# Seven output tiles on all 128 rows of the array, and batch 1's first transposes behind batch 0's last copies, in a fused attention and GeGLU kernel on one core

## Chip, cores, metric

One core of a Trainium2 chip. The metric is the device time of one execution in microseconds; less is better. In the profile's lines PE stands for TensorE's matmuls, PEld for its weight loads, DVE for VectorE and ACT for ScalarE; the span is the time from the first to the last instruction of the profiled execution, and a bank is the piece of accumulation memory that a group of matmuls fills before an engine copies it out.

## The reference, cut to what matters

```python
# q, k, v: (8, 12, 448, 64); w_gate, w_val: (768, 1536); w_out: (1536, 768)
scores = matmul(q, k.T) / sqrt(64)
x = matmul(maximum(scores, 0) ** 2 / 448, v)   # then (8 * 448, 768)
out = (gelu(x @ w_gate) * (x @ w_val)) @ w_out # (3584, 768), float32
```

## The kernel before: the parts that matter

The kernel lays out all work beforehand. Each piece is an `Op` with an engine, a planned cost and what it waits for; `run_plan` then issues the pieces in the order that the plan gives. TensorE has two queues in the plan: `PE0`, the lower 64 rows of the array, and `PE1`, the upper 64. On the chip they are one stream of instructions.

```python
def mm(o, lhsT, rhs, row, col, start, stop):           # a 64*64 tile of the array
    return nc.tensor.matmul(o, lhsT, rhs, start=start, stop=stop,
                            tile_position=(P * row, P * col))     # P = 64

def both(at, ops, step=0.0):         # lower and upper at the same time
    for i, (lo, hi) in enumerate(ops):
        lower.append((at + i * step, lo)); pairs.append(("with", lo, hi))

def then(at, step, los, his, done):  # the upper half of a bank after its lower half
    for i, lo in enumerate(los):
        lower.append((at + i * step, lo))
    pairs.append(("then", los[-1], his))
    bank_of[los[-1]] = done
```

The gate, value and output matmuls contract over 128 rows, but do it in two halves: the lower 64 rows accumulate into a bank, and when they are through, the upper 64 add theirs to the same bank, while the lower rows go on with the next bank. So at any time four 64*64 tiles can be at work on two banks. The upper rows lag by a bank or so. An output tile (128 of the 3584 rows, `FC` = 12 contraction steps, two column groups of 384):

```python
def emit(r, fc):
    if not box:
        box[0] = new_bank(cp)
    i, o = divmod(fc, WOG)
    if r == 1 and fc == 0:
        wait_lower(box)
    for j, (b, c) in enumerate(chunks):
        ins = mm(box[0][HALF[j], 0:N], uT[b][HALF[r], fc, c * P:(c + 1) * P],
                 wo[i][HALF[r], o, cols], r, j, r == 0 and fc == 0, r == 1 and fc == FC - 1)
    box[1] = ins
# ... [cut: the copy to osb on ACT, the stores]
ops = [[Op(f"PE{r}", step, lambda r=r, fc=fc: emit(r, fc), ...) for fc in range(FC)] for r in range(2)]
then(at, step, *ops, cp)
```

And where the upper halves go in the order:

```python
for kind, lo, hi in pairs:
    if kind == "with":
        upper.append((tau[place[lo]], hi))
    else:
        behind = place[lo] + 1
        # ... [cut: at least 0.3 us of lower work in between]
        hi[0].after = PE0[behind]
        t = tau[behind + 1]
        for i, op in enumerate(hi):
            if i:
                op.after = hi[i - 1]
            upper.append((t, op))
            t += op.cost
upper.sort(key=lambda w: w[0])
```

Attention is spread over this as scores (`sp`, 64*64 tiles), relu on ACT, square on VectorE, and products with v. For batches 0 and 1 q and k are transposed on TensorE by 128*64 tiles (line 334), and copied to `qkT` by VectorE. In the first batch, short of work, TensorE runs fillers of 128*128 (line 296).

## Time and profile before

| | before |
|---|---|
| median time | 430.91 us (430.79 to 432.42, 3 runs) |
| span of the profiled run | 428.7 us |
| TensorE busy | 419.9 us, 98% |
| from the span's start to batch 0's first gate matmul | 27.6 us |
| from there to batch 7's first gate matmul | 346.9 us |
| from there to the end ("the tail") | 54.2 us |

The last three rows cut the span at two instructions: the first gate matmul of batch 0 and that of batch 7. They are stages: start, middle, tail.

### The profile page before, as it was taken

Reading aid. Unit: us, or ns where it says so; the run is one execution under the profiler, and the core shown is the slowest. Engines: PE = TensorE matmul, PEld = TensorE weight load, DVE = VectorE, ACT = ScalarE, POOL = GpSimd, SP = SyncE. Lnnn points to the kernel's source line nnn. Section 1 sums busy time; section 2 is a strip of 40 time slices with the busy share of each in tenths; the row PEclk is TensorE's granted clock in tenths of the full one; section 3 lists DMA queues with packets and bytes.
Section 4 is the critical chain, followed back from the end, with each engine's and each line's share of the span. In section 5 each row is a group of like instructions: output and inputs, shape, how many; then the busy total and the mean of one; then the engine's idle time right before and its main releaser. Section 6 shows DMA issues by size and latency. Waiting matters only on the chain.

```text
span 428.7 us, 19594 instructions
## 1 busy us (share of the span) xinstructions
PE 419.9 (98%) x9091; PEld 359.7 (84%) x9094; DVE 211.1 (49%) x343; ACT 224.5 (52%) x323; POOL 71.6 (17%) x117
## 2 busy tenths in 40 slices
PE   8999999899999999999999999999999999999995
PEld 3559778678898888989999988979999978977895
DVE  3966666167544674347633675346633555212200
ACT  5937563366655555556455565565555565222221
POOL 8655420123001130023100230012200000000000
PEclk9999999999999999999999999999999999999999
DMA  8999999999434796379923699358932100220034
GB/s 109 196 199 198 202 208 185 185 134 140 73 84 90 93 151 75 75 109 140 127 58 95 89 133 118 76 85 109 151 71 77 38 4 3 53 63 3 2 78 112
DMA packets 75377, 44.91 MB, mean 105 GB/s; under 512 B 36128, under 2 KB 71840, under 8 KB 75296
## 3 DMA queue, kind: packets, MB, share of 16 engines
q0 software_dynamic: 37088, 24.39, 43.2%
q1 hardware_dynamic: 37968, 19.08, 26.2%
q8 instruction: 71, 1.16, 1.1%
q10 hardware_dynamic: 240, 0.20, 0.2%
q14 instruction: 10, 0.08, 0.1%
HBM read 48.76 MB, written 11.01 MB: 139 GB/s over the span
## 4 chain that ended last, share of the span: by engine, by line
PE 94%; DVE 2%; ACT 1%; issue 1%; DMA 1%; ACTq 0%; POOL 0%; POOLq 0%
PE ff L159 85%; PE sp L159 7%; ACT rl L381 1%; PE ff L296 1%; PE sp L334 1%; DMA qk<-in_k_dram 1%; DVE attnT L387 1%; DVE xT L437 1%; PE ff L334 0%; DVE qkT L338 0%; ACT osb L532 0%; ACTq L537 0%; POOL qk L211 0%; POOL table L148 0%; ACTq L381 0%
## 5 line engine op out<-in xcount | busy, mean ns | idle before, releaser
L159 PE MATMUL ff<-xT,wg 64*64 64x448 bf16 x2304 | 218.8, 349 | 0.2 <-DVE xT L437 0.2
L159 PE MATMUL ff<-xT,wv 64*64 64x448 bf16 x2304 | 217.6, 349 | 1.4 <-issue 1.4
L381 ACT ACTIVATE rl<-sp 128x896 bf16<-128x896 f32 x168 | 152.3, 918 | 98.2 <-PE sp L159 80.9
L159 PE MATMUL ff<-wo,uT 64*64 64x384 bf16 (+1 forms) x2736 | 150.6, 320 | 0.0
L159 PEld LDWEIGHTS <-wv 64*64 64x64 bf16 x2304 | 126.5, 107 | 18.4 <-issue 3.9
L387 DVE TENSOR_TENSOR attnT<-rl 128x896 bf16<-128x896 bf16 x168 | 104.0, 623 | 74.3 <-ACT rl L381 72.8
L159 PEld LDWEIGHTS <-wg 64*64 64x64 bf16 x2304 | 126.4, 107 | 16.3 <-issue 1.2
L159 PEld LDWEIGHTS <-uT 64*64 64x64 bf16 x2736 | 124.7, 107 | 5.3 <-issue 0.2
L159 PE MATMUL sp<-qkT 64*64 64x448 bf16 (+1 forms) x768 | 107.9, 328 | 0.6 <-ACT rl L381 0.4
L481 DVE TENSOR_TENSOR uT<-gel,ff 128x448 bf16<-128x448 bf16 x96 | 59.5, 620 | 77.0 <-PE ff L159 66.4
L159 PE MATMUL ff<-attnT,v 64*64 64x448 bf16 (+1 forms) x768 | 85.8, 327 | 0.1
L476 ACT ACTIVATE gel<-ff 128x448 bf16<-128x448 f32 x96 | 52.1, 543 | 51.2 <-PE ff L159 50.2
L532 ACT COPY osb<-ff 128x384 f32<-128x384 f32 (+1 forms) x57 | 26.8, 471 | 50.8 <-PE ff L159 47.6
L159 PEld LDWEIGHTS <-qkT 64*64 64x64 bf16 x768 | 43.1, 106 | 10.0 <-issue 3.8
L159 PEld LDWEIGHTS <-v 64*64 64x64 bf16 x768 | 44.6, 107 | 5.5 <-issue 1.2
L437 DVE TENSOR_SCALAR xT<-ff 128x448 bf16<-128x448 f32 x48 | 29.9, 623 | 32.0 <-PE ff L159 31.8
L211 POOL DMA_DIRECT2D qk<-in_q_dram x25 | 15.6, 622 | 152.5 <-DVE uT L481 146.0
L224 POOL DMA_DIRECT2D v<-in_v_dram x44 | 27.3, 628 | 32.7 <-DVE uT L481 24.0
L211 POOL DMA_DIRECT2D qk<-in_k_dram x25 | 15.4, 615 | 41.4 <-DVE uT L481 29.7
L258 DVE COPY qkr<-qk 128x1792 bf16<-128x1792 bf16 x18 | 19.3, 1078 | 0.0
L334 PEld LDWEIGHTS <-qk 128*64 128x64 bf16 x168 | 5.0, 109 | 3.0 <-issue 2.7
L338 DVE COPY qkT<-ff 128x896 bf16<-128x896 bf16 x6 | 3.7, 621 | 6.1 <-PE ff L334 6.1
(22 smaller groups left out, 39.5 us busy)
## 6 DMA issues: line engine op xcount, KB each, us to landing
out_dram<-osb SPq DMA_DIRECT2D x54, 192.0 KB, 2.7
v<-in_v_dram POOLq DMA_DIRECT2D x42, 128.0 KB, 6.2
qk<-in_q_dram POOLq DMA_DIRECT2D x23, 224.0 KB, 4.7
qk<-in_k_dram POOLq DMA_DIRECT2D x23, 224.0 KB, 5.0
wg<-in_moe_w_gate_dram POOLq DMA_DIRECT2D x6, 384.0 KB, 10.4
wv<-in_moe_w_val_dram POOLq DMA_DIRECT2D x6, 384.0 KB, 11.6
wo<-in_moe_w_out_dram POOLq DMA_DIRECT2D x4, 576.0 KB, 14.9
v<-in_v_dram POOLq DMA_DIRECT2D x2, 384.0 KB, 10.7
```

The lines of the kernel that those rows point to most:

```text
L159: return nc.tensor.matmul(o, lhsT, rhs, start=start, stop=stop, tile_position=(P * row, P * col))
L211: op = load(4 * (h1 - h0) * S * D, lambda: nc.gpsimd.dma_start(tile_of().rearrange("p (h x) -> p h x", h=H)[:, h0:h1, :], src[b, h0:h1].re ...
L224: return nc.gpsimd.dma_start(v16[b][HALF[i], h0:h1, :, :], v[b, h0:h1].rearrange("h (p c) d -> p h c d", c=SC)[:, :, c0:c0 + VC, :])
L258: nc.vector.tensor_copy(qkr[b][:, m], qk16[b].rearrange("p (h c d) -> p c h d", c=SC, d=D)[:, :, 4 * m:4 * m + 4])
L296: nc.tensor.matmul(t[:, :], warm[:, 0:128], warm[:, :], start=True, stop=True)
L334: nc.tensor.transpose(t[HALF[j], c, :], src[:, 2 * (2 * m + r) + j, c, :], ident[:, :], tile_position=(0, P * j))
L381: nc.scalar.activation(rl[:, :, :], box[0][:, :, 0:S], AF.Relu)
L387: nc.vector.tensor_tensor(a[:, :, :], box[1][:, :, :], box[1][:, :, :], op=ALU.mult)
L437: nc.vector.tensor_scalar_mul(xT[b][:, pr, :], box[0][:, 0:S], scalar1=out_scale)
L476: nc.scalar.activation(gel[b, fc][:, :], box[0][:, 0:S], AF.Gelu)
L481: u_op[b, fc].ins = nc.vector.tensor_tensor(uT[b][:, fc, :], gel.pop((b, fc))[:, :], box[0][:, 0:S], op=ALU.mult).ins
L532: nc.scalar.copy(ob[:, cols], box[0][:, 0:N])
```

## The change

Its intent: where no attention work stands beside the output tiles, an output matmul can use all 128 rows at once. This halves its instructions, needs no lag between halves, and lets a bank be finished and copied at once. And batch 1's first transposes, whose copies VectorE made between batch 0's last copies, come 3 us later, while batch 0's own transposes come a little earlier.

```diff
+        def emit_full(fc):
+            if not box:
+                box[0] = new_bank(cp)
+            i, o = divmod(fc, WOG)
+            for j, (b, c) in enumerate(chunks):
+                nc.tensor.matmul(box[0][HALF[j], 0:N], uT[b][:, fc, c * P:(c + 1) * P],
+                                 wo[i][:, o, cols], start=fc == 0, stop=fc == FC - 1,
+                                 tile_position=(0, P * j))
+        full = 0 < t < SC // 2 or 2 * t + 2 > SC * (B - 1) - 2      # tiles 1, 2 and 23 to 27
+        if full:
+            ops = [[Op("PE0", step, lambda fc=fc: emit_full(fc), ...) for fc in range(FC)],
+                   [Op("PE1", step, lambda: None) for _ in range(FC)]]
+            for lo, hi in zip(*ops):
+                hi.after = lo
 ... [cut: else as before]
-        then(at, step, *ops, cp)
+        if full:
+            both(at, zip(*ops), step)
+        else:
+            then(at, step, *ops, cp)
-    LO1 = 2.0
+    LO1 = 5.0
-                    x = (1.5 * step if rs == (1,) else -3.0) if b == 0 else -5.0 if m else -2.0
+                    x = ((0.5 if m else 1.5) * step if rs == (1,) else -4.6) if b == 0 else -5.0 if m else -2.0
```

More of the change, by code (lines that the diff above doesn't have):

```diff
@@ L537, in emit_store @@
             engine.dma_start(rows[c, :, cols], osb[t][HALF[j], cols])
-        ops = [[Op(f"PE{r}", step, lambda r=r, fc=fc: emit(r, fc),
+        def emit_full(fc):
[8 more added lines that the diff above has]
+        if full:
+            ops = [[Op("PE0", step, lambda fc=fc: emit_full(fc),
+                       [wo_op[fc // WOG], *(u_op[b, fc] for b, _ in chunks),
+                        *(ring_dep() if fc == 0 else ())], lag=0.24)
+                    for fc in range(FC)],
+                   [Op("PE1", step, lambda: None) for _ in range(FC)]]
+            for lo, hi in zip(*ops):
+                hi.after = lo
+        else:
+            ops = [[Op(f"PE{r}", step, lambda r=r, fc=fc: emit(r, fc),
                    [wo_op[fc // WOG], *(u_op[b, fc] for b, _ in chunks),
@@ L542, in add_out @@
                 for fc in range(FC)] for r in range(2)]
-        cp = Op("ACT", 0.48, emit_copy, [ops[1][-1]], prio=1)
+        cp = Op("ACT", 0.48, emit_copy, [ops[0 if full else 1][-1]], prio=1)
         ring.append(cp)
@@ L551, in add_out @@
                       for j in range(2))
-        then(at, step, *ops, cp)
+        if full:
+            both(at, zip(*ops), step)
+        else:
+            then(at, step, *ops, cp)
     for h0, h1 in ((0, 2), (2, 4), (4, 8), (8, 12)):
```

## The prediction

> **What bounds the kernel now.** I read the page first: its span, busy shares and chain of waits say which engine sets the time.
>
> ```profile
> span 428.7 us, 19594 instructions
> PE 419.9 (98%) x9091; PEld 359.7 (84%) x9094; DVE 211.1 (49%) x343; ACT 224.5 (52%) x323; POOL 71.6 (17%) x117
> ...
> PE ff L159 85%; PE sp L159 7%; ACT rl L381 1%; PE ff L296 1%; PE sp L334 1%; DMA qk<-in_k_dram 1%; DVE attnT L387 1%; DVE xT L437 1%; PE ff L334 0%; DVE qkT L338 0%; ACT osb L532 0%; ACTq L537 0%; POOL qk L211 0%; POOL table L148 0%; ACTq L381 0%
> ```
>
> TensorE is busy nearly always, and its matmuls are 93% of the chain. So what counts is how the array is packed. Almost every matmul is a 64*64 tile: four fit at once, two on the lower 64 rows and two on the upper. The lower rows run one bank's first half of the contraction while the upper rows run the second half of the bank before. I then asked for groups by shape on TensorE, for what the changed instructions cost today:
>
> ```profile
> L159 PE MATMUL ff<-wo,uT 64*64 64x384 bf16 x2640 | 149.5, 323 | 0.0
> L159 PE MATMUL ff<-wo,uT 64*64 64x192 bf16 x96 | 4.4, 243 | 0.0
> ```
>
> No idle time stands before them. Their cadence shows in the timeline of the tail, where only output tiles run: ACT copies a finished bank every 1.95 us (412.46, 414.41, 416.36), and a bank is 24 lower and 24 upper matmuls side by side. So a step of four matmuls takes 1.95 / 12 = 0.1625 us. The end of that timeline:
>
> ```profile
> 421.76 2.30 PE L159 MATMUL ff<-wo,uT 64*64 64x192 bf16 x45
> 423.23 0.48 ACT L532 COPY osb<-ff 128x384 f32<-128x384 f32 x1 [2.57 <-PE ff L159]
> 423.74 0.56 ACTq L537 DMA_DIRECT2D out_dram<-osb  x1
> 424.34 0.32 ACT L532 COPY osb<-ff 128x192 f32<-128x192 f32 x1 [0.63 <-PE ff L159]
> 424.68 0.50 ACTq L537 DMA_DIRECT2D out_dram<-osb  x1
> 425.22 0.32 ACT L532 COPY osb<-ff 128x192 f32<-128x192 f32 x1 [0.57 <-ACT osb L532]
> ```
>
> The last upper matmuls run alone until 424.06, with half the array empty. The last copy then starts only at 425.22, behind the copy and DMA issue of the piece before it. Last, the few places where the shape of the tile already changes, in the timeline of 25.8 to 28.0 us (start, duration, what):
>
> ```profile
> 25.89 0.48 PE L159 MATMUL ff<-attnT,v 64*64 64x448 bf16 x6
> 26.30 0.58 PE L334 MATMUL sp<-ident,qk 128*64 128x128 bf16 x14
> 26.82 0.38 PE L159 MATMUL ff<-attnT,v 64*64 64x448 bf16 x2
> 27.12 0.58 PE L334 MATMUL sp<-ident,qk 128*64 128x128 bf16 x14
> 27.63 0.38 PE L159 MATMUL ff<-attnT,v 64*64 64x448 bf16 x2
> ```
>
> Here one upper pair of 448 columns stands between two sets of full-row transposes. A pair in a stretch of one shape takes 0.189 us and a transpose pair about 0.055. From the start of the last transpose pair of the first set (26.66 in the records) to the next set is 0.46 us. Of that 0.055 + 0.19 is streaming; the rest, about 0.21, is two changes of shape, and the second pair after a change comes another 0.025 late. I call it 0.12 us per change. The records show 43 such changes, with a median of 0.096 us between the end of one stream and the next start, before the 0.025.
>
> **What the Trainium skill says.** "TensorEngine Tiling (Array Packing)", Key Properties: "Changing tiling mode (not just tile) drains the TensorE". The trace agrees: 0.12 us at each change, between 64*64, 128*64 and 128*128 alike. "TensorE: Matmul & The Clock Gate", the table under "Why this matters for your kernels", says that a matmul of 32 rows takes the time of one of 128. So a full-row pair should take what a half-row pair takes; the trace agrees as far as it can: in the warm-up 128*64 pairs of 512 columns follow each other by 0.216 us, which scaled to 384 is 0.162.
>
> **The change, part by part.** It has three: seven output tiles (1, 2 and 23 to 27) in 128*64; the plan start of batch 1's attention 3 us later, so that its first transposes come after batch 0's last copies; batch 0's transposes a little earlier.
>
> Full rows, streaming: a step of a full tile is two matmuls of 0.1625 us instead of four beside each other in 0.1625 us. The instruction count falls by 360, the streaming time by nothing. So this part can gain only at the edges.
>
> Full rows, changes of shape: this is where I looked hardest. I took both orders of TensorE's instructions and marked each place where the tile's shape changes: 45 before, 121 after. Around tile 1 there are 34 new ones, around tile 2 22, in the tail 22, at the start 2 fewer. The reason is the lag: when a full tile begins, the upper rows still owe a bank, and the planner deals those upper pairs one by one between the full pairs. Tile 23's first steps read: full pair, upper pair of gate, full pair, upper pair of gate, three full pairs, and so on. 76 x 0.12 = +9.1 us, all on the path, since nothing else may run in a change.
>
> Full rows, half-empty array: in such a stretch an upper pair runs alone. Around tile 1 some 15 pairs x 0.1625 = 2.4 us; around tile 2 some 6 x 0.19 = 1.1; in the tail 11 x 0.189 = 2.1, against the final stretch of the kernel before, 22 pairs of 192 columns at some 0.0825 = 1.8, which goes. Together 2.4 + 1.1 + 0.3 = 3.8, of which I take 3.5, as some drains overlap.
>
> The end: with full rows the last three pieces finish one after the other, the last 0.99 us after the one before, so that piece's copy (0.32) and issue (0.50) are done when the last is ready. The 425.22 - 424.06 = 1.16 us from last matmul to last copy shrinks to the 0.28 that a copy takes to see its matmul: -0.9 us.
>
> The start: before, VectorE takes the first two qkT copies of batch 1 (27.75 and 28.82, 0.62 each) between the last xT copies of batch 0 (28.29 and 29.35), and the last gate step waits until 30.02. Between 28.5 and 30.0 each half of the array starts only two pairs. After, these transposes (some 1.1 us with their changes) stand behind, so that step could come some 1.8 us earlier; the 1.1 us is paid later. That nets 0.7 us. The planner puts five fewer fillers of 0.216 in the first batch (17 against 22), so its planned gaps shrink by 1.1 us; I believe most of it, since ACT's relus there show 1.2 us of gaps. Start: -1.5 us.
>
> One more item is luck: at 76.55 us the array stands for 1.15 us for nothing that the profile shows ("issue"). It may go or stay; -0.4 on average.
>
> Sum: 9.1 + 3.5 - 0.9 - 1.5 - 0.4 = +9.8 us. 430.9 + 9.8 = 440.7; I say 440.5, a ratio of 1.022.
>
> **The rivals.** First, the changes of shape are cheaper in this setting: a change may cost only because transposes and fillers wait for other things as well. Then 76 changes at 0.05 are 3.8 us, and the time is about 435. Against it: the 0.092 to 0.119 us gaps are the same for three shapes, for lengths from 128 to 512 columns, and with or without a semaphore. At no cost at all it would be 430.9 + 3.5 - 2.8 = 431.6.
>
> Second, the start gives more than I count, since every microsecond of the attention chain there moves the whole kernel: 3 to 4 us instead of 1.5, thus about 438.5. For it: TensorE is only 93% busy from 20 to 30 us, ACT 51%. Against: TensorE's true idle there is 0.66 us, and the rest must be won from half-empty stretches.
>
> Third, weight loads bind the tail, and half the instructions make it quicker: the load row is 10.00 of 10 us busy from 410 to 420. Against: 0.1625 us per step is what the 128*64 warm-up pairs give per column, with far fewer loads. At best nothing changes.
>
> Fourth, the copies of full banks or the arrival of late uT tiles stall full steps, since they come in tile order without the other half's slack. Tile 24 needs the last uT, whose upper pair stands some 14 full steps earlier (2.3 us, against about 1 us for the product and its wait), so I expect none; if it came, 1 us more.
>
> **Range and chances.** The uncertain terms: 0.12 per change by a fifth, 1.8 us; the half-empty array 1 us; the start 1 us; the stall 0.6. Together some 2.4 us, a little more on the fast side, since the first two rivals both go that way: 436.0 to 443.5. The 2% line is 430.91 x 1.02 = 439.5, under my centre by 1.0: slower by over 2% 0.60, within 2% 0.39. Faster by over 2% would need 8.6 us, and TensorE's idle time in all is 8.8, most of it the launch and the last store: 0.01.
>
> **What would show it.** In the profile after: 128*64 rows for wo,uT with 360 matmuls in place of 720, and around 400 to 415 us alternating single pairs with starts about 0.28 to 0.31 us apart where today they are 0.16; the tail's copies spaced 1.95 us once no gate pair is left; the stretch from batch 1's first gate step to batch 7's last of the same length as before; batch 1's first gate step some 5 us later than today's, batch 2's some 8; the last copy 0.3 us behind the last matmul. Wrong would be: single pairs at 0.16 to 0.19 us between starts, so no cost for a change; or a first gate bank more than 3 us earlier.

## The result, and the profile after

The changed kernel takes 442.0 us (median of 6 runs, 441.15 to 443.22) against 431.5 (6 runs): 1.0244 times, interval 1.0220 to 1.0269, so slower. Ratios here and below are the mean time of one kernel's runs over that of the other's runs of the same rounds, so not quite the ratio of the medians.

The page after: span, busy shares, and the chain of waits by line (other lines left out):

```profile
span 439.6 us, 18865 instructions
PE 431.1 (98%) x8726; PEld 348.9 (79%) x8729; DVE 211.4 (48%) x343; ACT 224.4 (51%) x323; POOL 71.6 (16%) x117
...
PE ff L159 78%; PE sp L159 7%; PE ff L544 7%; DVE attnT L387 2%; DMA qk<-in_k_dram 1%; DVE xT L437 1%; PE sp L334 1%; POOL qk L211 1%; DVE qkT L338 0%; ACT osb L532 0%; PE ff L334 0%; ACTq L537 0%; PE ff L296 0%; ACT rl L381 0%; POOL ident masks.py:199 0%
```

TensorE is "busy" for 98% again, with 365 matmuls fewer and 11 us more. Busy time doesn't show what was lost: a matmul's recorded time (some 323 ns for 384 columns) is about double the 0.1625 us after which the next on the same rows starts, so short gaps between streams vanish in it. The groups by shape show the new instructions, each at nearly the mean duration of the old (332 against 323 ns for 384 columns, 246 against 243 for 192). The old groups are smaller by the 720 that they replace, 624 of 384 columns and all 96 of 192:

```profile
L159 PE MATMUL ff<-wo,uT 64*64 64x384 bf16 x2016 | 121.6, 323 | 0.0
...
L544 PE MATMUL ff<-wo,uT 128*64 128x384 bf16 x312 | 32.8, 332 | 0.0
...
L544 PE MATMUL ff<-wo,uT 128*64 128x192 bf16 x48 | 2.1, 246 | 0.0
```

Where the time is lost shows in the order. The timeline of TensorE after, at the beginning of the tail (start us, duration us, line, what):

```profile
412.05 0.35 PE L544 MATMUL ff<-wo,uT 128*64 128x384 bf16 x2
412.33 0.38 PE L159 MATMUL ff<-xT,wg 64*64 64x448 bf16 x2
412.64 0.35 PE L544 MATMUL ff<-wo,uT 128*64 128x384 bf16 x2
412.92 0.38 PE L159 MATMUL ff<-xT,wg 64*64 64x448 bf16 x2
413.23 0.68 PE L544 MATMUL ff<-wo,uT 128*64 128x384 bf16 x6
413.84 0.38 PE L159 MATMUL ff<-xT,wg 64*64 64x448 bf16 x2
```

A full pair starts 0.28 us before the upper gate pair that follows it, and that one 0.31 us before the next full pair. In a stretch of one shape they would be 0.16 and 0.19 apart, and today's upper gate pair would run beside lower work, not alone. Taken from the records, after 60 us there are 78 changes of shape, with together 8.55 us between the end of one stream and the next start (median 0.116; a stream is taken to last 0.417 ns per column, about the 0.42 at which pairs of one shape follow each other). The kernel before has none there.

The end of the kernel after:

```profile
434.15 0.48 ACT L532 COPY osb<-ff 128x384 f32<-128x384 f32 x1 [1.51 <-PE ff L544]
435.26 0.32 ACT L532 COPY osb<-ff 128x192 f32<-128x192 f32 x1 [0.63 <-PE ff L544]
435.61 0.50 ACTq L537 DMA_DIRECT2D out_dram<-osb  x1
435.98 0.14 PEld L159 LDWEIGHTS <-warm 64*64 64x64 bf16 x4
435.98 0.25 PE L159 MATMUL sp<-warm 64*64 64x64 bf16 x4
436.14 0.32 ACT L532 COPY osb<-ff 128x192 f32<-128x192 f32 x1 [0.57 <-PE ff L544]
```

The last output matmul ends at 436.05 in the records and the last copy starts at 436.14: 0.09 us, where the kernel before had 1.16. Banks finish one after the other, and no copy waits behind another copy's store.

The stages (one profiled execution each; the last column is TensorE's idle after 40 us, in pieces over 0.1 us, that the profile puts down to nothing, "issue"):

| kernel | start | middle | tail | unexplained idle |
|---|---|---|---|---|
| before | 27.6 | 346.9 | 54.16 | 1.4 |
| after | 26.5 | 357.8 | 55.28 | 1.1 |

So the start is 1.1 us shorter, the middle 10.9 us longer and the tail 1.1 us longer. (One execution's start is worth little: the nine traces below and here with the old start have 27.6 to 29.1 us, and the kernel before happens to have the least.)

### The profile page after: what moved, and what is told of

The parts are those of the page before. It is cut to its first block, busy times and chain, and to the rows that moved or that the text cites. A ratio compares the mean times of both kernels' runs of the same rounds, so it can differ in the third digit from the quotient of the medians.

```text
span 439.6 us, 18865 instructions
## 1 busy us (share of the span) xinstructions
PE 431.1 (98%) x8726; PEld 348.9 (79%) x8729; DVE 211.4 (48%) x343; ACT 224.4 (51%) x323; POOL 71.6 (16%) x117
## 4 chain that ended last, share of the span: by engine, by line
PE 93%; DVE 3%; DMA 1%; POOL 1%; issue 1%; ACT 0%; ACTq 0%; POOLq 0%
PE ff L159 78%; PE sp L159 7%; PE ff L544 7%; DVE attnT L387 2%; DMA qk<-in_k_dram 1%; DVE xT L437 1%; PE sp L334 1%; POOL qk L211 1%; DVE qkT L338 0%; ACT osb L532 0%; PE ff L334 0%; ACTq L537 0%; PE ff L296 0%; ACT rl L381 0%; POOL ident masks.py:199 0%
## 5 line engine op out<-in xcount | busy, mean ns | idle before, releaser
L159 PE MATMUL ff<-xT,wg 64*64 64x448 bf16 x2304 | 222.2, 349 | 1.5 <-issue 1.1
L159 PE MATMUL ff<-xT,wv 64*64 64x448 bf16 x2304 | 222.1, 350 | 0.0
L159 PEld LDWEIGHTS <-wv 64*64 64x64 bf16 x2304 | 127.8, 107 | 19.6 <-issue 4.3
L159 PEld LDWEIGHTS <-wg 64*64 64x64 bf16 x2304 | 127.7, 107 | 19.0 <-issue 2.9
L159 PE MATMUL ff<-wo,uT 64*64 64x384 bf16 x2016 | 121.6, 323 | 0.0
L159 PE MATMUL sp<-qkT 64*64 64x448 bf16 (+1 forms) x768 | 106.1, 328 | 0.9 <-ACT rl L381 0.8
L159 PEld LDWEIGHTS <-uT 64*64 64x64 bf16 x2016 | 95.5, 107 | 8.9 <-issue 4.6
L159 PE MATMUL ff<-attnT,v 64*64 64x448 bf16 (+1 forms) x768 | 86.7, 327 | 0.1
L544 PE MATMUL ff<-wo,uT 128*64 128x384 bf16 (+1 forms) x360 | 34.8, 321 | 0.0
L544 PEld LDWEIGHTS <-uT 128*64 128x64 bf16 x360 | 17.8, 109 | 12.8 <-issue 8.0
```

Of the source, the lines that this page charges most:

```text
L544: nc.tensor.matmul(box[0][HALF[j], 0:N], uT[b][:, fc, c * P:(c + 1) * P], wo[i][:, o, cols], start=fc == 0, stop=fc == FC - 1, tile_positi ...
```

## The experiments

Theory: a change of the tile's shape costs TensorE some 0.12 us each, an upper pair between full-row steps runs alone, and these two make the time. Rivals: changes are nearly free, and the lost overlap or the dealt-out order costs; or the moved attention work costs. A third came from the trace after: the start's gain is smaller than predicted, since batch 0's third set of transposes now waits for its load.

Every kernel was run beside the kernel before on the same chip. Each result is correct unless it says otherwise. The stages of their profiled executions:

| kernel | median, before beside it | ratio (95%) | start | middle | tail | unexplained idle |
|---|---|---|---|---|---|---|
| rows_only | 440.92, 431.22 | 1.0222 (1.0184 to 1.0261) | 28.9 | 354.6 | 55.26 | 0.2 |
| shifts_only | 430.84, 431.22 | 0.9982 (0.9950 to 1.0013) | 26.5 | 349.1 | 54.14 | 0.9 |
| rows_drained | 434.20, 431.22 | 1.0065 (1.0025 to 1.0105) | 28.8 | 350.2 | 52.89 | 0.3 |
| tail_mixed | 432.91, 431.22 | 1.0038 (0.9994 to 1.0083) | 29.1 | 347.0 | 55.25 | 0.8 |
| tail_drained | 430.14, 431.13 | 0.9960 (0.9926 to 0.9994) | 28.1 | 346.5 | 52.91 | 1.2 |
| tail_quads | 429.95, 431.13 | 0.9961 (0.9918 to 1.0004) | 28.6 | 345.8 | 53.92 | 0.9 |
| dose_change | 436.56, 431.13 | 1.0116 (1.0066 to 1.0165) | 28.8 | 346.4 | 58.80 | 0.6 |
| dose_same | 431.27, 431.13 | 0.9987 (0.9942 to 1.0033) | 28.2 | 348.0 | 53.60 | 2.5 |
| lo1_only | 431.07, 432.00 | 1.0005 (0.9965 to 1.0045) | 27.1 | 348.2 | 54.14 | 0.4 |
| x_only | 432.00, 432.00 | 1.0003 (0.9982 to 1.0024) | 28.2 | 348.0 | 54.12 | 2.0 |
| lo1_tail_drained | 430.39, 432.00 | 0.9967 (0.9939 to 0.9994) | 27.1 | 348.8 | 52.85 | 0.7 |
| tail26_drained | 430.63, 431.09 | 0.9986 (0.9966 to 1.0007) | 28.7 | 349.1 | 53.23 | 3.6 |

The tail is the quiet stage: four kernels that leave it as it was (before, shifts_only, lo1_only, x_only) have 54.12 to 54.16. Start and middle carry the noise of a single execution. The load that batch 0's third set of transposes needs lands at 10.4 us in the kernel before, the earliest, and at up to 12.0 in others; the first 14 transposes take 0.58 us there and 0.96 in rows_only; and idle that the profile doesn't explain comes and goes, all of it in the middle. Taking that idle off makes the middles agree: the seven kernels that leave start and middle as they were (before, the three tail kernels, the two dose kernels, tail26_drained) then have 345.0 to 346.2.

A difference of some tenths of a per cent is claimed below only where the tail shows it too.

The unexplained idle itself has a pattern in the traces. One DMA queue carries instructions (from the kernel before, queue: packets, MB, share):

```profile
q8 instruction: 71, 1.16, 1.1%
```

That is 71 packets of 16 KB, one for every 256 of TensorE's 18185 matmuls and weight loads. All 28 pieces of this idle in the 14 traces stand at the same place in a row of 128 matmuls (the 86th to 92nd by the records, some of which are missing), and each ends 1.3 to 2.2 us after such a packet landed. Without a pause it is more: over all packets of the kernel before, the median from landing to the matmul at that place is 4.0 us. In the kernel before, the packet in front of the 1.15 us landed at 76.17 and TensorE went on at 77.70. So this idle looks like instructions that come late. No run varied it: this is a reading of the records, not an experiment.

### The parts alone: rows_only and shifts_only

rows_only undoes the moves, shifts_only the full rows:

```diff
 # rows_only
-    LO1 = 5.0
+    LO1 = 2.0
 # ... and x as before
 # shifts_only
-        full = 0 < t < SC // 2 or 2 * t + 2 > SC * (B - 1) - 2
+        full = False
```

> The seven full-row tiles alone, both moves of the attention undone. Order: 76 more changes of shape than in the kernel before (54 around tiles 1 and 2, 22 in the tail). Theory (a change costs 0.12 us, an upper pair alone its whole 0.16 to 0.19): +9.1 + 3.5 - 0.9 = about +11.7 us, 443. Rival (the moves of the attention cost the time, or part of it): well under +10.9, say +5 or less.

> The two moves of the attention alone, no full-row tile. Predicted gain 1.5 us, so 429.5. The trace after makes me doubt it: the third set of transposes now waits 1.2 us for its load and the first batch's last product is no earlier, so 0 to -0.5 us. Rival (the moves cost): +3 us or more.

The full rows alone cost about what the whole change costs, 9.7 us by the medians (1.0222) against 10.5 (1.0244). The moves alone are within noise of nothing, 0.9982. The rival that blames the moves falls. The gain of 1.5 us that the prediction gave them isn't seen, though the interval, 0.9950 to 1.0013, would still hold it; the section on the start looks closer.

### The same full-row steps with few changes: rows_drained

A full tile's first step now waits until the upper rows have paid all they owe, and a bank's twelve full steps stand together. Nothing else is different from rows_only.

```diff
-            both(at, zip(*ops), step)
+            both(at, zip(*ops))            # one bank's full steps side by side
 ...
+    firsts = [i for i, op in enumerate(PE0) if op in full_ops and PE0[i - 1] not in full_ops]
+    for _, lo, his in pairs:
+        if lo not in full_ops:
+            for i in firsts:
+                if place[lo] < i:
+                    PE0[i].deps.append(his if isinstance(his, Op) else his[-1])
+                    break
 # [cut: full_ops gathers the full steps; an upper half whose lower one stands just before a full step waits for that lower one alone]
```

> As rows_only, but a full tile starts only when the upper rows have paid their debt, and a bank's twelve full steps stand together: 10 late changes of shape instead of 76, the same full-row matmuls, the same lone upper pairs. Theory: 66 x 0.12 = 8 us faster than rows_only, so about +3.5 us over the kernel before. Rival (a change is nearly free, the half-empty array and the lost overlap cost): within 2 us of rows_only.

10 late changes instead of 76 and 440.92 - 434.20 = 6.7 us less: 0.10 us per change. By stage the tail is shorter by 55.26 - 52.89 = 2.37 for 20 changes, 0.118 each, and the middle by 354.6 - 350.2 = 4.4 for 46, 0.10 each; there the new order also moves lower work, so that the 0.10 is less clean. The rival that changes are nearly free falls. What is left in the middle, without the unexplained idle, is 349.9 us against 345.0 to 346.2: 3.8 to 5.0 us for tiles 1 and 2. Eight changes there are 1.0 of it; the rest, 2.8 to 4.0 us, is then the half-empty array, as far as a difference of single executions can tell. The same sum for rows_only, which has the dealt-out order itself, is 354.4 less 345.0 to 346.2 less 54 x 0.12, or 1.8 to 3.0 us.

### The tail alone: tail_mixed, tail_drained, tail_quads

Only tiles 23 to 27 are full, and the start is as before: once in the dealt-out order, once drained, and once in the dealt-out order but with each full step made of four 64*64 matmuls, whose upper two write a bank that nobody reads. The last gives a wrong result (relative error 0.30).

```diff
 # tail_mixed
-        full = 0 < t < SC // 2 or 2 * t + 2 > SC * (B - 1) - 2
+        full = 2 * t + 2 > SC * (B - 1) - 2
 # tail_drained: tail_mixed with the edit of rows_drained
 # tail_quads: tail_mixed with
-            for j, (b, c) in enumerate(chunks):
-                nc.tensor.matmul(box[0][HALF[j], 0:N], uT[b][:, fc, c * P:(c + 1) * P], ...
+            if fc == 0:
+                box[1] = psS.tile([128, 2, 512], f32, name="sp", tag="S")
+            for r in range(2):
+                for j, (b, c) in enumerate(chunks):
+                    dst = box[1][HALF[j], 0, 0:N] if r else box[0][HALF[j], 0:N]
+                    mm(dst, uT[b][HALF[r], fc, c * P:(c + 1) * P], wo[i][HALF[r], o, cols], r, j, ...
```

> Only tiles 23 to 27 in full rows, in the dealt-out order, start as before. 22 late changes. Theory: 22 x 0.12 + 0.3 - 0.9 = +2.0 us by the sum of the prediction; the trace after shows +1.1 from batch 7's first gate on, so +1 to +2. Rival (the tail gains, blocks 1 and 2 lose all): below 0.

> Only tiles 23 to 27 in full rows, begun when the upper rows have paid: 2 late changes instead of tail_mixed's 22, start as before. Theory: 20 x 0.12 = 2.4 us under tail_mixed, so -0.8 to -1.2 us against the kernel before (the tail of rows_drained gained 1.2 from batch 7's first products on). Rival (a change is nearly free): within 0.5 us of tail_mixed, +1 to +1.6.

> As tail_mixed in order, but each full-row step is four 64*64 matmuls at once, the upper two into a bank that nobody reads: the result is wrong on purpose. The same lone upper pairs, no change of shape. Theory: 22 changes less, 2.6 us under tail_mixed, so about -1 us against the kernel before. Rival (dealing single upper pairs between steps costs, whatever the shape): as tail_mixed, +1.6.

tail_mixed costs 1.7 us by the medians and 1.09 in its tail; tail_drained wins 1.25 in its tail and 0.4% in all. The same full-row matmuls thus cost or gain, by the order alone. The timeline of tail_drained (TensorE and ACT) shows the single change and the even pace behind it:

```profile
402.05 0.73 PE L159 MATMUL ff<-xT,wg 64*64 64x448 bf16 x6
...
402.62 0.35 PE L159 MATMUL ff<-xT,wv 64*64 64x448 bf16 x2
402.80 0.35 PE L159 MATMUL ff<-xT,wg 64*64 64x448 bf16 x2
402.99 0.35 PE L159 MATMUL ff<-xT,wv 64*64 64x448 bf16 x2
403.18 0.35 PE L159 MATMUL ff<-xT,wg 64*64 64x448 bf16 x2
403.37 0.92 PE L159 MATMUL ff<-xT,wv 64*64 64x448 bf16 x8
...
404.22 19.72 PE L545 MATMUL ff<-wo,uT 128*64 128x384 bf16 x264
...
406.40 0.48 ACT L533 COPY osb<-ff 128x384 f32<-128x384 f32 x1 [2.28 <-PE ff L545]
408.35 0.48 ACT L533 COPY osb<-ff 128x384 f32<-128x384 f32 x1 [1.47 <-PE ff L545]
...
424.03 0.32 ACT L533 COPY osb<-ff 128x192 f32<-128x192 f32 x1 [0.56 <-PE ff L545]
```

Ten gate and value pairs run alone, 0.19 us apart in the records, from 402.24 on; then, from 404.22 on, a bank takes 1.95 us, the pace of the kernel before. So half the instructions stream no faster. The last output matmul ends 49.35 us after batch 7's first gate matmul, against 49.53 before; the other 1.07 us of the gain is the end, where the last copy starts 0.09 us behind that matmul and not 1.16.

tail_quads keeps tail_mixed's order without its changes of shape, and is 3.0 us faster by the medians. Its tail is only 1.3 us shorter, since the DMA issue in front of its last copy took 1.80 us where the other kernels have some 0.50:

```profile
422.73 0.32 ACT L532 COPY osb<-ff 128x192 f32<-128x192 f32 x1 [0.63 <-PE sp L159]
...
423.08 1.80 ACTq L537 DMA_DIRECT2D out_dram<-osb  x1
...
424.92 0.32 ACT L532 COPY osb<-ff 128x192 f32<-128x192 f32 x1 [1.87 <-issue]
```

The copy before it, which that issue does not touch, starts 48.30 us after batch 7's first gate matmul, against 50.94 in tail_mixed: 2.64 us less, the 22 x 0.12 of the theory. But four free 64*64 tiles also let a lower pair run ahead beside a lone upper one, so this run takes away a part of the half-empty array as well. The next pair is the cleaner proof.

### A dose of changes: dose_change and dose_same

tail_drained with a small pair (64 columns, result unread) after 22 of tile 25's full steps: in 64*64, or, as a control, in the 128*64 of the steps around it.

```diff
+            if t == 25 and fc < FC - 1:
+                if fc == 0:
+                    box[1] = psS.tile([128, 2, 512], f32, name="sp", tag="S")
+                for j in range(2):
+                    mm(box[1][HALF[j], 0, 0:P], warm[HALF[0], 0:P], warm[HALF[0], 0:P], 0, j, True, True)
 # dose_same, in place of mm:
+                    nc.tensor.matmul(box[1][HALF[j], 0, 0:P], warm[:, 0:P], warm[:, 0:P],
+                                     start=True, stop=True, tile_position=(0, P * j))
```

> tail_drained with a pair of 64*64 matmuls of 64 columns, results unread, after 22 of tile 25's 24 full steps: 44 changes of shape more. Theory: 44 x 0.12 + 22 x 0.027 = +5.9 us over tail_drained, with starts about 0.43 us apart from full step to full step. Rival (a change is hidden behind the streaming of a full step): under +1.5 us.

> The control: the same 22 small pairs, in 128*64 as the steps around them, so no change more than tail_drained. Both: 22 x 0.027 = +0.6 us, at most +1 if short matmuls cost a little of their own.

TensorE's timeline in dose_change:

```profile
418.25 0.22 PE L159 MATMUL sp<-warm 64*64 64x64 bf16 x2
418.40 0.35 PE L545 MATMUL ff<-wo,uT 128*64 128x384 bf16 x2
418.68 0.22 PE L159 MATMUL sp<-warm 64*64 64x64 bf16 x2
418.83 0.35 PE L545 MATMUL ff<-wo,uT 128*64 128x384 bf16 x2
```

and in dose_same:

```profile
416.51 0.20 PE L552 MATMUL sp<-warm 128*64 128x64 bf16 x2
416.54 0.33 PE L545 MATMUL ff<-wo,uT 128*64 128x384 bf16 x2
416.70 0.20 PE L552 MATMUL sp<-warm 128*64 128x64 bf16 x2
416.73 0.33 PE L545 MATMUL ff<-wo,uT 128*64 128x384 bf16 x2
```

From small pair to small pair it is 0.43 us with changes and 0.19 without: (0.43 - 0.19) / 2 = 0.12 us per change. Over the tail, (58.80 - 53.60) / 44 = 0.118; over the medians, (436.56 - 431.27) / 44 = 0.120. Against tail_drained the tail is 5.89 us longer, where 5.9 was expected. The control's own cost is (53.60 - 52.91) / 22 = 0.03 us per pair, its streaming. This settles the cost of a change, in ordinary matmuls, with no wait near.

### The start: lo1_only and x_only

```diff
 # lo1_only: no full rows, x as before
     LO1 = 5.0
 # x_only: no full rows, LO1 = 2.0, x as in the change
```

> Only batch 1's attention 3 us later in the plan, batch 0's transposes as before, no full rows. Theory (my prediction's step): batch 0's last products some 1.5 us earlier, paid back in part by the later transposes, net -0.7 us. Rival (what is gained at 28 us is spent before batch 1's first gate): -0.3 to +0.3.

> Only batch 0's transposes earlier. Theory from the trace after: the third set, now ahead of two score units in TensorE's order, waits 0.8 to 1.2 us for its load, which the fewer gaps behind it give back: -0.3 to +0.5 us. My prediction's step (five fewer fillers are 1.1 us won): -0.8 us.

Neither shows a change: 1.0005 and 1.0003. The times alone would not exclude the 0.7 us predicted for lo1_only (its mean holds one run of 435.77 us; its median is 0.9 below that of the kernel before), so the stages have to decide. Start and middle together, without the unexplained idle, are 374.9 us in lo1_only, 374.2 in x_only and 374.7 in shifts_only; the seven kernels that leave both stages as they were have 373.1 to 375.2. With full rows it is 383.2 after against 383.3 in rows_only. No gain is left by batch 7. Both mechanisms are there all the same. In lo1_only VectorE makes the two last xT copies back to back, and the last ends at 29.06 instead of 29.96, although this execution's attention runs 0.97 us later than in the kernel before from its seventh relu on:

```profile
27.77 1.29 DVE L437 TENSOR_SCALAR xT<-ff 128x448 bf16<-128x448 f32 x2 [0.95 <-PE ff L159]
```

That is the 1.8 us that the prediction gave this step. But the middle is then 348.2 us with only 0.4 unexplained, against 346.9 with 1.4: 2.3 us given back. The records show most of it: 28 transposes moved there, in 14 pairs of 0.055, 0.8; eight more changes of shape in the middle (14 against 6), 1.0; and one filler, 0.2. In x_only TensorE waits for a load in front of the third set of transposes, which now stands ahead of work that was ready:

```profile
9.75 0.38 PE L159 MATMUL sp<-qkT 64*64 64x448 bf16 x4
11.31 0.58 PE L334 MATMUL ff<-ident,qk 128*64 128x128 bf16 x14 [1.18 <-DMA qk<-in_k_dram]
```

Its seventh relu is 1.4 us behind before's, its last 0.5 us: the fewer fillers give 0.9 back. A part of the 1.4 is chance: that load landed at 10.4 us in the kernel before and at 11.2 in x_only, and lo1_only, with the old place of this set, also waits 0.91 us for it (landed at 11.5).

### A version that beats both, and whether it holds: lo1_tail_drained, tail26_drained

lo1_tail_drained is tail_drained with `LO1 = 5.0`. tail26_drained makes only the last two tiles full:

```diff
-        full = 2 * t + 2 > SC * (B - 1) - 2
+        full = 2 * t + 4 > SC * B - 2
```

> Candidate for a version that beats both: tail_drained with batch 1's attention 3 us later. If the parts add: -1.6 us (0.996) with lo1_only's gain of a few tenths, so -1.2 to -2.3. If lo1 is neutral: as tail_drained.

> tail_drained with the last two tiles alone in full rows, to see whether its gain holds. The upper rows now pay 12 pairs of 384 columns (1.95 us) instead of 12 of 448 (2.27): up to 0.3 us less than tail_drained, so -1.0 to -1.5 us against the kernel before. Rival (tail_drained's gain is chance or comes from more full-row steps): 0, or half of it.

lo1_tail_drained has the drained tail again, 52.85 us, and 0.9967: as tail_drained, so moving batch 1's attention adds nothing. tail26_drained was a miss: I expected 0.3 us more than tail_drained, and its tail has 0.3 less, 53.23. I had counted the debt that tail_drained pays as 12 pairs of 448 columns. Its records show ten alone, since two still find a partner, 1.9 us; tail26_drained enters between two output banks, where 13 pairs of 384 columns run alone (25 matmuls in one row of 2.27 us on its timeline, from 417.16 on), 2.1 us. That accounts for 0.2 of the 0.3. Its profiled execution, the longest of its six, holds 3.6 us of unexplained idle. The best version here is tail_drained: 430.14 us, 0.9960 times the kernel before. Three kernels with its tail (tail_drained, lo1_tail_drained, rows_drained) have 52.85 to 52.91 there, so its 1.3 us are no chance; but they are 0.3% of the kernel.

## Why the prediction was right

- **Changes of shape: right.** 76 more in the order, 78 of them late and 2 fewer at the start (the trace shows the 78 after 60 us), 0.12 us each, +9.1. The dose gives 0.118 to 0.120; the 66 changes taken out by rows_drained gave 6.7 us. This agrees with the drain that "TensorEngine Tiling (Array Packing)", Key Properties, states, also between ordinary matmuls in a full stream.
- **Streaming of a full step: right.** A bank still takes 1.95 us; 360 matmuls instead of 720 gain nothing. The rival of load-bound weights falls. So does the stall on late uT tiles: TensorE is 10.00 of 10 us busy from 410 to 420 and from 420 to 430.
- **Half-empty array, tiles 1 and 2, 2.4 + 1.1 = 3.5 us: right in kind, its size not pinned.** The remainder is 1.8 to 3.0 us in rows_only and 2.8 to 4.0 in rows_drained, whose lone pairs are not all the same. Both are differences of single executions.
- **The tail: its sum was too high.** 22 x 0.12 + 0.3 - 0.9 = 2.0 predicted, 1.1 measured. The changes are as predicted (22 with 2.4 us of gaps in tail_mixed) and the end gains 1.07 instead of 0.9. The mis-sized term is the lone pairs: +0.3 predicted, 1.1 - 2.6 + 1.07, about -0.4, measured. In part it is a misread line: the row of 45 matmuls in 2.30 us in the prediction gives the shape of its first matmul, and the records show four pairs of 384 columns among those of 192. That lone stretch is 2.2 us, not 1.8. The other 0.3 us stays open.
- **The start, -1.5 us: wrong.** Nothing is left of it by batch 7: shifts_only 0.9982 with an interval across 1, both halves 1.000, and start and middle together no shorter than in the kernels without the moves. The rival that the start gives more than 1.5 us falls with it. The copies did come earlier as said, and the start is shorter (26.5 us in both traces with both moves, 27.6 to 29.1 in the nine without); the middle gave it back. The prediction counted 1.1 us for the moved transposes there, and the middle of lo1_only is 2.3 longer. The fewer fillers counted as 1.1 us won; a filler marks a planned gap, and a wait for a load took its place in part.
- **The unexplained idle, -0.4: it stayed, at another place.** 1.15 us at 76.5 us before, 1.07 at 271 us after, each ending some 1.5 us after an instruction packet landed. The packet that was late before was as late after (both landed at 76.17 us), but TensorE ran 101 matmuls from 70 to 80 us and not 203, so it did not need the packet yet. On TensorE's timeline before:

```profile
77.70 0.38 PE L159 MATMUL ff<-xT,wv 64*64 64x448 bf16 x2 [1.15 <-issue]
```

and after:

```profile
272.10 0.35 PE L159 MATMUL ff<-xT,wg 64*64 64x448 bf16 x1 [1.07 <-issue]
```

The sum, +9.8 us, met 10.5 by medians of the same rounds. That it met it so closely is luck in part: errors of 0.9 too high in the tail and about 2 too hopeful at the start and for the idle partly cancelled. Of the stated signs, batch 2's first gate matmul came 8.6 us later than before (some 8 predicted), batch 1's 6.8 (some 5), and the last copy 0.09 us behind the last matmul (0.3). One did not hold: from batch 1's first gate matmul to batch 7's first it is 302.8 us against 299.9, not the same length. It could not have been, with batch 2 put 3 us further back than batch 1; from batch 2's on it is 246.4 against 245.3.

## What to carry to other kernels

Before mixing tile shapes on TensorE, count in the issued order how often the shape changes: each costs about 0.12 us here whatever the two shapes are, which is most of a step's streaming, and busy time doesn't show it. A shape that is free in a long stretch must be entered once, after the other shape's debts are paid; a planner that knows only durations may deal the two out one by one, as this one did. And a gain at a chain's start is worth only what is left of it a stage later: mark one instruction in each stage and compare those.

## What the Trainium skill lacked or had wrong

- "TensorEngine Tiling (Array Packing)", Key Properties, has the drain at a change of tiling mode, but no cost. These runs: about 0.095 us from the end of one stream to the next start and about 0.025 more before the second pair, 0.118 to 0.120 us per change in all (dose_change against dose_same), the same for streams of 64 to 512 columns and among 64*64, 128*64 and 128*128.
- The same page does not mention the second loss that mixed shapes bring: a tile of half the rows has no partner between full-row steps. Here an upper gate pair took 0.31 us from its start to the next full step's, 0.12 for the change and 0.19 of streaming that before ran beside lower work.
